# Segment sums on VectorE from transposed rows instead of on TensorE, with the average values and memory rows one token block later

## The chip, the core and the metric

The kernel runs on one core of a Trainium2 chip. Its engines work in parallel, each through its own instruction queue in order: TensorE (matmuls), VectorE, ScalarE, GpSimd, and SyncE, which here only issues DMA transfers (GpSimd issues some too). The metric is the device time of the whole kernel in microseconds (us). Tiles on the chip have 128 partitions; matmul results land in PSUM and are emptied from there by VectorE or ScalarE.

## What is computed

The input x has 2048 tokens of 1024 features. With xn = layernorm(x), the output is the sum of x, a recurrent attention over xn, and an MLP over xn:

```python
xn = _layernorm(x)
return x + _A_ref(xn, mem0, Wq, Wk, Wv, Wo, 32) + _B_ref(xn, w1, w2, w3, w4)
# _A_ref: 64 segments of 32 tokens, one after the other
mem = mem0                                  # 8 memory rows
for s in range(64):
    h = concat([mem, xs[s]])                # 40 rows: memory, then the segment
    o = attention(h @ Wq, h @ Wk, h @ Wv) @ Wo      # 32 heads of 128, causal mask on the segment
    mem = o[:8]; outs.append(o[8:])
# _B_ref: token-mixing MLP, then a plain one
h  = gelu(layernorm(xn) @ w1);  x1 = xn + shift(h) @ w2
return x1 + gelu(layernorm(x1) @ w3) @ w4   # w3: 1024 x 3584
```

The loop over segments is serial as written. The kernel breaks it by an approximation that it verifies at its end: a memory row attends to all 40 rows almost evenly, so the memory of the next segment is close to the average of the 40 values, projected by Wo. For that it needs, ahead of the attention, the sum over the 32 tokens of each segment of xn: 64 sums of 1024 features. From these come the average values (a product with Wv) and from them the memory rows (a product with Wo).

## The kernel before

Four stages follow each other, and TensorE's order is the order of the code (a manual schedule).

1. *First matmul of the token mixing* (lines 171 to 350; about 1.5 to 69 us). 16 tiles of 128 tokens, taken in pairs. For each tile VectorE makes statistics and a normalised copy `xn2`, a DMA transpose (`dma_trans`, L234) or TensorE (`pe_trans`, L252) turns it to features on partitions, and TensorE multiplies it with w1 (`stage1`, `w1_part`, L265; `single`, L294). `normalise_x` (L244, ScalarE) overwrites the loaded x by xn, in place. `seg_sums` (L257 to L261) runs two tiles behind it: it takes the tile's xn, 128 tokens on partitions, as stationary operand in 8 slices of 128 features, against a constant 128 x 4 matrix of zeros and ones (`segone`), which yields the sums of its four segments; ScalarE copies them to `xs`.
2. *Second matmul of the token mixing* (L357 to L386; 69 to 125 us): w2, the residual x1, its statistics, `xn3` and its transposes `xn3Ts` (four tiles of 512 tokens, in the buffers tagged x0 to x3). x1 goes to memory as `R1`.
3. *MLP* (L388 to L578; 125 to 528 us). A loop over four blocks `tb` of 512 tokens. Each has a first phase of 28 groups of 8 matmuls with w3 (L553; ScalarE empties PSUM with the gelu, L554), and a second phase of 8 groups of 28 matmuls with w4 (L571; VectorE empties PSUM, L572, by adding into `R1`). All groups of both phases share one ring of four PSUM tiles (`mm_tile`). `load_R1(n)` (L475) brings R1 and x of tile n back; GpSimd adds x to R1; VectorE makes xn of x (L481), and GpSimd stores xn to memory (`xn_d`, L482), from where the attention will load it transposed. The x tile of this comes from a ring of two buffers, tag `xt`.
   Between the groups, `filler(tb, ph, i)` runs the work of the average values: 16 chunks of 1 MB of weights, 8 of Wv (`psvb`, L425) and 8 of Wo (`psG`, L446), at the places of the dictionary `plan`. A chunk is loaded by SyncE when the one before it in its buffer has been used (buffer x0 for the Wv chunks; x0 and x1 for the Wo chunks). `xb` (L402, L403) holds the segment sums as the moving operand for Wv; its first column includes mem0. The last chunk ends in the memory rows `MZ` (L449), which the attention subtracts from x (`make_xm`, L517) and projects (`mem_proj`).
4. *Attention* (from L580; 528 us to the end): 32 steps of projections, scores, values, and the output projection (L834).

Of the kernel before, what the change touches and what calls it, by code (L numbers as in the profile page):

```python
# [13 lines left out]
BF16 = mybir.dt.bfloat16  # L14
F32 = mybir.dt.float32
I32 = mybir.dt.int32
ALU = mybir.AluOpType
ACTF = mybir.ActivationFunctionType
AX = mybir.AxisListType
PSUM = bass.MemoryType.PSUM  # L20

P = 128
S = 2048
D = 1024
KT = D // P
NT = S // P
# [5 lines left out]
M = 8  # L32
SEG = 32
# [3 lines left out]
NG = NSEG - 1  # L37
# [26 lines left out]
def kernel(  # L64
# [16 lines left out]
    nc = tc.nc  # L81
    x_v = A_x[0].rearrange("(n p) d -> p n d", p=P)
# [14 lines left out]
    xn_d = tc.dram_tile([S, D], BF16, name="xn_scratch")  # L97
    xn_v = xn_d.rearrange("(n p) d -> p n d", p=P)
# [3 lines left out]
    def const_tile(name, arr, dt=BF16, later=False):  # L102
        a = _bf(arr) if dt == BF16 else np.asarray(arr, np.float32)
        d = nc.inline_tensor(a, name=name)
        t = cpool.tile(list(arr.shape), dt, name=name + "_sb")
        load = lambda: nc.gpsimd.dma_start(t[:], d.ap())
        if later:
            return load, t
        load()
        return t  # L110
# [11 lines left out]
    load_segone, segone = const_tile("c_segone", segone_np, later=True)  # L122
# [14 lines left out]
    def aux_tile(shape, tag, name):  # L137
        return psum.tile(shape, F32, tag=tag, bufs=1, name=name)
# [4 lines left out]
    spec = specx.enter_context(tc.tile_pool(name="spec", bufs=1))  # L143
    xs = spec.tile([P, KT, NSEG], F32)
    xb = spec.tile([P, KT, NG], BF16)
    m0 = spec.tile([M, D], BF16)
    lnst = spec.tile([P, NT, 4], F32)

    rightx = main.enter_context(ExitStack())
# [14 lines left out]
    with ExitStack() as keepx:  # L164
        keep = keepx.enter_context(tc.tile_pool(name="keep", bufs=1))
        w2_sb = keep.tile([P, KT, D], BF16)
        xts = [keep.tile([P, D], BF16, name=f"x{n}") for n in range(NT)]
# [3 lines left out]
        with ExitStack() as p0:  # L171
            big = p0.enter_context(tc.tile_pool(name="p0big", bufs=1))
            ring = p0.enter_context(tc.tile_pool(name="p0ring", bufs=3))
# [69 lines left out]
            def normalise_x(n):  # L243
                nc.scalar.activation(xts[n][:], xts[n][:], ACTF.Identity, bias=nms.pop(n)[:], scale=lnst[:, n, 2:3])  # L244
# [9 lines left out]
                        w = 2 if n == 0 else 4  # L254
                        nc.scalar.copy(xn2Ts[n // 2][:, n % 2, 4 * h + q:4 * h + q + w, :], p3_[:, q:q + w, :])

            def seg_sums(n):  # L257
                ps = aux_tile([P, KT, 4], "AB"[n % 2], "psX")
                for k in range(KT):
                    nc.tensor.matmul(ps[:, k, :], xts[n][:, k * P:(k + 1) * P], segone[:], start=True, stop=True)  # L260
                nc.scalar.copy(xs[:, :, 4 * n:4 * n + 4], ps[:])  # L261

            def w1_part(g, co, ps, ks):
                for k in ks:
                    nc.tensor.matmul(ps, w1_sb[:, k, co * P:(co + 1) * P], xn2Ts[g][:, :, k, :], start=(k == 0), stop=(k == KT - 1))  # L265
                if ks[-1] == KT - 1:
                    nc.scalar.activation(hTB[:, co, 2 + g * 256:2 + g * 256 + 256], ps, ACTF.Gelu_apprx_tanh)
# [21 lines left out]
            def single(n, b):  # L289
                ps = mm_tile("ps1")[:].rearrange("p (c t) -> p c t", c=4)  # L290
                for c in range(4):
                    co = 4 * b + c
                    for k in range(KT):
                        nc.tensor.matmul(ps[:, c, :], w1_sb[:, k, co * P:(co + 1) * P], xn2Ts[n // 2][:, n % 2, k, :], start=(k == 0), stop=(k == KT - 1))  # L294
                gelu4(n, b, ps)
# [30 lines left out]
            ln_apply(4)  # L326
            dma_trans(4)
            single(3, 0)
            seg_sums(0)
            seg_sums(1)  # L330
            normalise_x(2)
            ln_stats(6)
            ln_apply(5)
# [3 lines left out]
            for g in range(2, NT // 2):  # L337
                nxt = [n for n in (2 * g + 2, 2 * g + 3) if n < NT]
                for n in nxt:
                    if 6 < n + 1 < NT:  # L340
                        ln_stats(n + 1)
                    ln_apply(n)
                    dma_trans(n)
                stage1(g, range(4))
                for n in (2 * g, 2 * g + 1):
                    seg_sums(n - 2)
                    normalise_x(n)
                stage1(g, range(4, KT))
            seg_sums(NT - 2)
            seg_sums(NT - 1)  # L350

        x3_pool = rightx.enter_context(tc.tile_pool(name="x3", bufs=1, side="right"))
        w3b_pool = rightx.enter_context(tc.tile_pool(name="w3b", bufs=1, side="right"))
# [3 lines left out]
        with ExitStack() as p2:  # L357
            ring = p2.enter_context(tc.tile_pool(name="p2ring", bufs=4))
            for n in range(NT):
                x1 = ring.tile([P, D], F32, tag="x1", bufs=6)  # L360
                st = ring.tile([P, 2, 6], F32, tag="st")
                for ch in range(2):
                    ps = mm_tile("ps2")
# [7 lines left out]
                a = ring.tile([P, 1], F32, tag="a")  # L371
# [17 lines left out]
    with ExitStack() as p3:  # L389
        big = p3.enter_context(tc.tile_pool(name="p3big", bufs=1))  # L390
        ring = p3.enter_context(tc.tile_pool(name="p3ring", bufs=3))
        w4t = []
        for c in range(7):
            t = big.tile([P, 4, D], BF16, name=f"w4_{c}")
# [3 lines left out]
        ps9 = aux_tile([P, KT, M + 1], "B", "ps9")  # L398
        for k in range(KT):
            nc.tensor.matmul(ps9[:, k, :], m0[:, k * P:(k + 1) * P], eye9[:], start=True, stop=True)  # L400
        nc.vector.tensor_copy(MZ[:, :, 0:M], ps9[:, :, 0:M])
        nc.vector.tensor_tensor(xb[:, :, 0:1], ps9[:, :, M:M + 1], xs[:, :, 0:1], op=ALU.add)  # L402
        nc.vector.tensor_copy(xb[:, :, 1:NG], xs[:, :, 1:NG])  # L403

        chunks = {}

        def load_chunk(c, slot):
            t = x3_pool.tile([P, 8 * 512], BF16, tag=f"x{slot}", name=f"chunk{c}")
            if c < 8:
                nc.sync.dma_start(t[:].rearrange("p (k e) -> p k e", k=KT), Wv_v[:, :, c * 512:(c + 1) * 512])  # L410
            else:
                nc.sync.dma_start(t[:].rearrange("p (h d) -> p h d", h=4), Wo_v[:, (c - 8) * 4:(c - 7) * 4, :])
            chunks[c] = t
# [37 lines left out]
        plan = {}  # L451
        slots = {}
        for i in range(4):
            plan[(0, 1, 2 * i + 1)] = i
            plan[(1, 0, 7 * i + 6)] = 4 + i
            plan[(1, 1, 2 * i + 1)] = 8 + i
            plan[(2, 0, 7 * i + 6)] = 12 + i
        for c in range(16):
            slots[c] = 0 if c < 8 else c % 2

        def filler(tb, ph, i):
            c = plan.get((tb, ph, i))
            if c is None:
                return
            use_chunk(c)
            nx = c + 2 if c >= 8 else c + 1
            if c == 7:
                load_chunk(8, slots[8])
                load_chunk(9, slots[9])
            elif c < 7 or nx < 16:  # L470
                load_chunk(nx, slots[nx])
# [3 lines left out]
        def load_R1(n):  # L475
            R1 = ring.tile([P, D], F32, tag="R1", name="R1")
            nc.sync.dma_start(R1[:], R1_v[:, n, :])
            xt = ring.tile([P, D], BF16, tag="xt", name="xt", bufs=2)
            nc.sync.dma_start(xt[:], x_v[:, n, :])
            nc.gpsimd.tensor_tensor(R1[:], R1[:], xt[:], op=ALU.add)  # L480
            nc.vector.tensor_scalar(xt[:], xt[:], lnst[:, n, 0:1], lnst[:, n, 2:3], op0=ALU.subtract, op1=ALU.mult)  # L481
            nc.gpsimd.dma_start(xn_v[:, n, :], xt[:])  # L482
            R1s[n] = R1

        A = {}
# [62 lines left out]
        for tb in range(4):  # L548
            for f in range(FT):
                ps = mm_tile("ps3")  # L550
                w3 = w3a if f < FH else w3b
                for k in range(KT):
                    nc.tensor.matmul(ps[:], w3[:, k, (f % FH) * P:(f % FH + 1) * P], xn3Ts[tb][:, :, k, :], start=(k == 0), stop=(k == KT - 1))  # L553
                nc.scalar.activation(h3T[:, f, :], ps[:], ACTF.Gelu_apprx_tanh)  # L554
                filler(tb, 0, f)
                if f == 20:
                    load_R1(tb * 4)
            if tb == 0:
                load_chunk(0, 0)
            if tb == 3:  # L560
                rightx.close()
                att_open()
            for j in range(4):
                n = tb * 4 + j
                if j < 3:
                    load_R1(n + 1)
                R1 = R1s.pop(n)
                for ch in range(2):
                    ps = mm_tile("ps4")
                    for f in range(FT):  # L570
                        nc.tensor.matmul(ps[:], h3T[:, f, j * P:(j + 1) * P], w4t[f // 4][:, f % 4, ch * 512:(ch + 1) * 512], start=(f == 0), stop=(f == FT - 1))  # L571
                    nc.vector.tensor_tensor(R1[:, ch * 512:(ch + 1) * 512], ps[:], R1[:, ch * 512:(ch + 1) * 512], op=ALU.add)  # L572
                    filler(tb, 1, 2 * j + ch)
                nc.gpsimd.dma_start(R_v[:, n, :], R1[:])
                if tb == 3 and j == 0:
                    att_prep()
# [288 lines left out]
    for i in range(NS):  # L865
        s = new_step(i)
        p = steps.get(i - 1)
# [67 lines left out]
        if last:  # L935
            b = s.b
# [31 lines left out]
    with tc.If(cond > 0):  # L968
        with ExitStack() as fctx:
# [17 lines left out]
            with tc.For_i(0, NSEG, 1) as i:  # L987
# [7 lines left out]
                for hg in range(8):  # L995
# [8 lines left out]
                    ps = fps.tile([P, 4, L], F32, tag="mm")  # L1004
# [4 lines left out]
                    ps = fps.tile([P, 4, L], F32, tag="mm")  # L1009
# [4 lines left out]
                    ps = fps.tile([P, 512], F32, tag="mm")  # L1014
# [33 lines left out]
                for ch in range(2):  # L1048
                    ps = fps.tile([P, 512], F32, tag="op")
# [44 lines left out]
```

## Time and profile before

| what | number |
|---|---|
| time, median of 3 runs (lowest to highest) | 1485.37 us (1484.79 to 1486.12) |
| span of the profiled execution | 1481.8 us |
| TensorE busy | 1474.5 us |
| VectorE, ScalarE, GpSimd busy | 502.1, 346.9, 206.3 us |
| granted TensorE clock | full speed throughout |
| share of the DMA engines, block 0's second phase (173.65 to 225.83 us) | 0.53 |

How to read it: TensorE is busy nearly all the time, so the shares of the other engines say how much room lies beside it. The chain of waits follows the end of the kernel back to the start, at each step to what released it. In the rows of groups, the first number after the bar is the busy time in us, the second the mean of one in ns, and then comes the idle time of the engine before these instructions and what ended it. "DMA to landing" is the time from the issue of a transfer to its completion. A busy record of one matmul is longer than its slot, since matmuls are pipelined; the slot is read from the chain.

### The profile page before, as it was taken

The numbers are of one execution on the slowest core, as the hardware profiler recorded it, in microseconds if no ns is written. First come the engines' busy times: TensorE is split into PE (matmuls) and PEld (weight loads), VectorE is DVE, ScalarE is ACT, GpSimd is POOL, SyncE is SP. The second block draws the span as 40 slices with busy tenths as digits, with TensorE's granted clock in tenths as the row PEclk, the third lists the DMA queues.
The fourth block names the chain that finished last, engine by engine and source line by source line (L and its number), as shares of the span: only waits on it lengthen the run. The fifth ranks groups of instructions, "written<-read, shape, count | busy, mean of one in ns | idle before, by whom it ended". The sixth has DMA issues, their size and how long they took to land.

```text
span 1481.8 us, 28303 instructions
## 1 busy us (share of the span) xinstructions
PE 1474.5 (100%) x12400; PEld 758.2 (51%) x12400; DVE 502.1 (34%) x1025; ACT 346.9 (23%) x887; POOL 206.3 (14%) x482
## 2 busy tenths in 40 slices
PE   9999999999999999999999999999999999999998
PEld 8844444444444456666544444444444444444444
DVE  8283010010110213435441454540255432253443
ACT  6633202103113023333310232220122220032220
POOL 6152131211120201111100000000000000000000
PEclk9999999999999999999999999999999999999999
DMA  8599653454120735474531364541345452244301
GB/s 219 140 287 245 239 192 100 163 175 154 56 107 8 232 131 186 158 212 159 177 106 57 119 171 143 157 143 54 103 148 167 143 157 72 66 141 155 109 21 54
DMA packets 189184, 208.39 MB, mean 141 GB/s; under 512 B 50168, under 2 KB 157832, under 8 KB 189056
## 3 DMA queue, kind: packets, MB, share of 16 engines
q1 hardware_dynamic: 180768, 178.82, 40.3%
q0 software_dynamic: 8288, 27.72, 5.1%
q8 instruction: 99, 1.62, 0.5%
q14 instruction: 29, 0.24, 0.0%
HBM read 170.07 MB, written 25.17 MB: 132 GB/s over the span
## 4 chain that ended last, share of the span: by engine, by line
PE 99%; DMA 0%; SPq 0%; DVE 0%; issue 0%
PE psK L634 15%; PE psV L643 15%; PE psP L834 15%; PE psQ L616 15%; PE ps L553 13%; PE ps L571 13%; PE ps L366 4%; PE ps L265 3%; PE psS L667 1%; PE psO L697 1%; PE psM L652 1%; PE psvb L425 1%; PE psG L446 1%; PE ps L294 0%; DMA x<-in_A_x_dram 0%; PE ps L280 0%
## 5 line engine op out<-in xcount | busy, mean ns | idle before, releaser
L834 PE MATMUL psP<-wo_sb,oX 128*128 128x512 bf16 (+1 forms) x1056 | 222.2, 373 | 0.0
L571 PE MATMUL ps<-w,hT_all 128*128 128x512 bf16 x896 | 195.0, 379 | 0.0
L634 PEld LDWEIGHTS <-w 128*128 128x128 bf16 x1280 | 125.1, 98 | 99.1
L616 PE MATMUL psQ<-xT,w 128*128 128x512 bf16 x768 | 170.4, 379 | 0.0
L643 PE MATMUL psV<-w,xT 128*128 128x512 bf16 x768 | 170.3, 379 | 0.0
L634 PE MATMUL psK<-xT,w 128*128 128x512 bf16 x768 | 169.7, 379 | 0.0
L834 PEld LDWEIGHTS <-oX 128*128 128x128 bf16 x1056 | 103.2, 98 | 117.1
L616 PEld LDWEIGHTS <-w 128*128 128x128 bf16 x1024 | 98.8, 98 | 115.9
L635 ACT CAST K<-psK 128x512 bf16<-128x512 f32 (+1 forms) x160 | 80.3, 502 | 303.7 <-PE psK L634 303.7
L623 DVE TENSOR_TENSOR Q<-psQ,QM 128x512 bf16<-128x512 f32 (+1 forms) x128 | 87.3, 685 | 166.3 <-PE psQ L616 107.9
L644 ACT CAST V<-psV 128x512 bf16<-128x512 f32 x128 | 74.9, 585 | 289.6 <-PE psV L643 289.5
L571 PEld LDWEIGHTS <-hT_all 128*128 128x128 bf16 x896 | 87.2, 98 | 103.8
L554 ACT ACTIVATE hT_all<-ps 128x512 bf16<-128x512 f32 x112 | 66.8, 597 | 283.5 <-PE ps L553 283.5
L643 PEld LDWEIGHTS <-xT 128*128 128x128 bf16 x768 | 74.2, 98 | 84.7
L553 PE MATMUL ps<-xn3T,w3a 128*128 128x512 bf16 x448 | 97.7, 379 | 0.0
L553 PE MATMUL ps<-xn3T,w3b 128*128 128x512 bf16 x448 | 97.7, 379 | 0.0
L702 DVE TENSOR_TENSOR oX<-psE,VM 128x128 bf16<-128x128 f32 x32 | 9.3, 291 | 215.2 <-PE psE L698 215.2
L709 DVE TENSOR_TENSOR oX<-psO,VM 128x96 bf16<-128x96 f32 (+2 forms) x256 | 82.0, 391 | 0.0
L840 DVE TENSOR_TENSOR ot<-psP,Rt 128x512 bf16<-128x512 f32 (+1 forms) x33 | 22.3, 675 | 167.7 <-PE psP L834 164.8
L553 PEld LDWEIGHTS <-w3b 128*128 128x128 bf16 x448 | 43.6, 98 | 51.9
L553 PEld LDWEIGHTS <-w3a 128*128 128x128 bf16 x448 | 43.4, 98 | 51.8
L481 DVE TENSOR_SCALAR xt<-xt,lnst 128x1024 bf16<-128x1024 bf16 x16 | 8.7, 545 | 180.3 <-POOL R L480 180.3
(161 smaller groups left out, 1259.0 us busy)
## 6 DMA issues: line engine op xcount, KB each, us to landing
w<-in_A_Wq_dram SPq DMA_DIRECT2D x32, 1024.0 KB, 5.4
w<-in_A_Wk_dram SPq DMA_DIRECT2D x32, 1024.0 KB, 5.3
w<-in_A_Wv_dram SPq DMA_DIRECT2D x32, 1024.0 KB, 6.6
R_scratch<-x POOLq DMA_DIRECT2D x16, 512.0 KB, 7.5
R<-R_scratch SPq DMA_DIRECT2D x16, 512.0 KB, 7.0
chunk<-in_A_Wv_dram SPq DMA_DIRECT2D x8, 1024.0 KB, 5.4
R_scratch<-R POOLq DMA_DIRECT2D x16, 512.0 KB, 4.2
chunk<-in_A_Wo_dram SPq DMA_DIRECT2D x8, 1024.0 KB, 6.3
```

The costliest lines, as they stand in the source:

```text
L366: nc.tensor.matmul(ps[:], hTB[:, k, o:o + P], w2_sb[:, k, ch * 512:(ch + 1) * 512], start=(k == 0), stop=(k == KT - 1))
L553: nc.tensor.matmul(ps[:], w3[:, k, (f % FH) * P:(f % FH + 1) * P], xn3Ts[tb][:, :, k, :], start=(k == 0), stop=(k == KT - 1))
L554: nc.scalar.activation(h3T[:, f, :], ps[:], ACTF.Gelu_apprx_tanh)
L571: nc.tensor.matmul(ps[:], h3T[:, f, j * P:(j + 1) * P], w4t[f // 4][:, f % 4, ch * 512:(ch + 1) * 512], start=(f == 0), stop=(f == FT - 1))
L616: nc.tensor.matmul(ps[:], w[:, k, hh * P:(hh + 1) * P], s.xm[:, k, 0:512], start=(k == 0), stop=(k == KT - 1))
L623: nc.vector.tensor_tensor(q3[:, j0:16, 0:SEG], p3_[:, j0:16, :], QM[:, 4 * s.hg + hh, z + j0:z + 16].unsqueeze(2).to_broadcast((P, 16 - j0 ...
L634: nc.tensor.matmul(ps[:, 0:c], w[:, k, hh * P:(hh + 1) * P], s.xm[:, k, h2 * c:(h2 + 1) * c], start=(k == 0), stop=(k == KT - 1))
L635: nc.scalar.copy(s.K[:, hh, h2 * c:(h2 + 1) * c], ps[:, 0:c])
L643: nc.tensor.matmul(ps[:], s.xm[:, k, m * P:(m + 1) * P], w[:, k, :], start=(k == 0), stop=(k == KT - 1))
L644: nc.scalar.copy(s.V[:, m, :], ps[:])
L709: nc.vector.tensor_tensor(oX[:, h0:h0 + hn, :].rearrange("p h (m c) -> p m h c", c=P)[:, m0:m1, :, SEG * j:SEG * (j + 1)], o4[:, 4 * m0:4 ...
L834: nc.tensor.matmul(ps[:, 0:w], oX[:, h, m * P:(m + 1) * P], wo_sb[:, h, cc], start=(h == 0), stop=(h == H - 1))
```

## The change

The segment sums leave the first stage and TensorE. Instead, xn is made and stored in the first block and a half of the MLP stage, by a new function `make_xn` for each of the 16 tiles (load x, normalise on VectorE, store from GpSimd), apart from `load_R1`, which keeps its own load of x for the sum with R1. When four tiles are stored, `load_sum(b)` brings those 512 rows back by one DMA transpose from SyncE, with features on partitions and tokens along the free axis, into the buffer x0, which is free once block 0's first phase has ended. There VectorE sums 32 tokens at a time (`tensor_reduce`, four instructions of two feature slices each per block of 512). `last_sum` makes `xb` and starts the first chunk load. The average values begin one token block later (block 1's second phase instead of block 0's), and all later chunks move with them; the last one now lies in block 3's first phase. `m0s` keeps mem0's column sum until `xb` is made. The places in the schedule are given by the dictionary `prep`, whose keys are block, phase and group; `filler` runs what is there ahead of a chunk.

```diff
-            def seg_sums(n):
-                ps = aux_tile([P, KT, 4], "AB"[n % 2], "psX")
-                for k in range(KT):
-                    nc.tensor.matmul(ps[:, k, :], xts[n][:, k * P:(k + 1) * P], segone[:], start=True, stop=True)
-                nc.scalar.copy(xs[:, :, 4 * n:4 * n + 4], ps[:])
...
-        nc.vector.tensor_tensor(xb[:, :, 0:1], ps9[:, :, M:M + 1], xs[:, :, 0:1], op=ALU.add)
-        nc.vector.tensor_copy(xb[:, :, 1:NG], xs[:, :, 1:NG])
+        nc.vector.tensor_copy(m0s[:], ps9[:, :, M:M + 1])
...
-            plan[(0, 1, 2 * i + 1)] = i
-            plan[(1, 0, 7 * i + 6)] = 4 + i
-            plan[(1, 1, 2 * i + 1)] = 8 + i
-            plan[(2, 0, 7 * i + 6)] = 12 + i
+            plan[(1, 1, 2 * i + 1)] = i
+            plan[(2, 0, 7 * i + 6)] = 4 + i
+            plan[(2, 1, 2 * i + 1)] = 8 + i
+            plan[(3, 0, 7 * i + 6)] = 12 + i
...
+        def make_xn(n):
+            xt = ring.tile([P, D], BF16, tag="xt", name="xt", bufs=2)
+            nc.sync.dma_start(xt[:], x_v[:, n, :])
+            nc.vector.tensor_scalar(xt[:], xt[:], lnst[:, n, 0:1], lnst[:, n, 2:3], op0=ALU.subtract, op1=ALU.mult)
+            nc.gpsimd.dma_start(xn_v[:, n, :], xt[:])
+
+        def load_sum(b):
+            sums[b] = x3_pool.tile([P, KT * 512], BF16, tag="x0", name=f"xTs{b}")
+            nc.sync.dma_start_transpose(sums[b][:].rearrange("p (k t) -> p k t", k=KT), xn_d[b * 512:(b + 1) * 512, :])
+
+        def seg_sums(b, k0):
+            nc.vector.tensor_reduce(xs[:, k0:k0 + 2, 16 * b:16 * b + 16], sums[b][:].rearrange("p (k s i) -> p k s i", k=KT, i=SEG)[:, k0:k0 + 2, :, :], axis=AX.X, op=ALU.add)
+
+        def last_sum():
+            nc.vector.tensor_tensor(xb[:, :, 0:1], m0s[:], xs[:, :, 0:1], op=ALU.add)
+            nc.vector.tensor_copy(xb[:, :, 1:NG], xs[:, :, 1:NG])
+            load_chunk(0, 0)
...
+        for n in range(6):
+            do(0, 0, 10 + 3 * n, make_xn, n)
+        for n in range(6, 14):
+            do(0, 1, n - 6, make_xn, n)
+        do(1, 0, 0, make_xn, 14)
+        do(1, 0, 3, make_xn, 15)
+        for b, (load, sumat) in enumerate((((0, 1, 1), [(0, 1, 4)] * 4), ((0, 1, 5), [(1, 0, 1)] * 2 + [(1, 0, 2)] * 2),
+                                           ((1, 0, 3), [(1, 0, 10 + t) for t in range(4)]), ((1, 0, 14), [(1, 0, 22 + t) for t in range(4)]))):
+            do(*load, load_sum, b)
+            for t, pos in enumerate(sumat):
+                do(*pos, seg_sums, b, 2 * t)
+        do(1, 0, 26, last_sum)
...
         def load_R1(n):
...
             nc.gpsimd.tensor_tensor(R1[:], R1[:], xt[:], op=ALU.add)
-            nc.vector.tensor_scalar(xt[:], xt[:], lnst[:, n, 0:1], lnst[:, n, 2:3], op0=ALU.subtract, op1=ALU.mult)
-            nc.gpsimd.dma_start(xn_v[:, n, :], xt[:])
             R1s[n] = R1
```

Also removed are the calls of the old `seg_sums` in the first stage and, at the end of block 0's first phase, `load_chunk(0, 0)`, which `last_sum` now does.

More of the change, by code (lines that the diff above doesn't have):

```diff
@@ L146 @@
     m0 = spec.tile([M, D], BF16)
+    m0s = spec.tile([P, KT, 1], F32)
     lnst = spec.tile([P, NT, 4], F32)
@@ L328 @@
             single(3, 0)
-            seg_sums(0)
-            seg_sums(1)
             normalise_x(2)
@@ L345 @@
                 for n in (2 * g, 2 * g + 1):
-                    seg_sums(n - 2)
                     normalise_x(n)
                 stage1(g, range(4, KT))
-            seg_sums(NT - 2)
-            seg_sums(NT - 1)
         x3_pool = rightx.enter_context(tc.tile_pool(name="x3", bufs=1, side="right"))
@@ L453, with do @@
         for i in range(4):
-            plan[(0, 1, 2 * i + 1)] = i
-            plan[(1, 0, 7 * i + 6)] = 4 + i
-            plan[(1, 1, 2 * i + 1)] = 8 + i
-            plan[(2, 0, 7 * i + 6)] = 12 + i
+            plan[(1, 1, 2 * i + 1)] = i
+            plan[(2, 0, 7 * i + 6)] = 4 + i
+            plan[(2, 1, 2 * i + 1)] = 8 + i
+            plan[(3, 0, 7 * i + 6)] = 12 + i
         for c in range(16):
             slots[c] = 0 if c < 8 else c % 2
+        sums = {}
+        def make_xn(n):
[12 more added lines that the diff above has]
+            load_chunk(0, 0)
+        prep = {}
+        def do(tb, ph, i, f, *a):
+            prep.setdefault((tb, ph, i), []).append((f, a))
+        for n in range(6):
[10 more added lines that the diff above has]
+        do(1, 0, 26, last_sum)
         def filler(tb, ph, i):
+            for f, a in prep.get((tb, ph, i), ()):
+                f(*a)
             c = plan.get((tb, ph, i))
@@ L557 @@
                     load_R1(tb * 4)
-            if tb == 0:
-                load_chunk(0, 0)
             if tb == 3:
```

## The prediction

> **What bounds the kernel now.** I read the page's chain of waits first, to see which engine carries the end.
>
> ```profile
> PE 99%; DMA 0%; SPq 0%; DVE 0%; issue 0%
> PE psK L634 15%; PE psV L643 15%; PE psP L834 15%; PE psQ L616 15%; PE ps L553 13%; PE ps L571 13%; PE ps L366 4%; PE ps L265 3%; PE psS L667 1%; PE psO L697 1%; PE psM L652 1%; PE psvb L425 1%; PE psG L446 1%; PE ps L294 0%; DMA x<-in_A_x_dram 0%; PE ps L280 0%
> ```
>
> TensorE is the chain, end to end: its own waits add up to 2.7 us, nearly all at the start. So a matmul that is removed is worth its slot, and every new wait of TensorE is lost in full. Nothing else counts. Next I took the chain in order of time, in the first stage and then around block 0 of the MLP.
>
> ```profile
> 22.27 0.38 PE psX L260 x16
> 22.65 0.47 PE psT L252 x8
> ...
> 28.44 0.38 PE psX L260 x16
> 28.82 7.01 PE ps L265 x64
> 35.83 0.38 PE psX L260 x16
> ```
>
> Two tiles' segment sums (16 matmuls of 4 columns) take 0.38 us of the chain, 24 ns each. The 164 ns that the record of one gives is latency, not its slot.
>
> ```profile
> 173.65 12.09 PE ps L571 x56
> 185.74 0.96 PE psvb L425 x32
> ...
> 224.87 0.96 PE psvb L425 x32
> 225.83 9.28 PE ps L553 x43
> ```
>
> Block 0's second phase (eight groups of 28 matmuls, 6.05 us each) carries four average-value groups of 0.96 us.
>
> Last, the rows that price what is added: VectorE's sums along the free axis and its normalisation (groups by form), a 512-row transpose (the answer for its line), and loads and stores of one tile (the page's DMA issues).
>
> ```profile
> L676 DVE TENSOR_REDUCE ss<-EQ 128x16 f32<-128x528 f32 x32 | 22.5, 703 | 2.7
> L481 DVE TENSOR_SCALAR xt<-xt,lnst 128x1024 bf16<-128x1024 bf16 x16 | 8.7, 545 | 180.3 <-POOL R L480 180.3
> L503 SPq DMA_TRANSPOSE xT<-xn_scratch x4: 3970/6436/8562, 479.0 to 1106.6; - x4
> DMA to landing us min/median/max: 6.0/8.6/12.1
> Rt<-R_scratch SPq DMA_DIRECT2D x32, 256.0 KB, 2.9
> xn_scratch<-xt POOLq DMA_DIRECT2D x16, 256.0 KB, 2.3
> ```
>
> [...] 528 elements 703 ns, 16 elements 170 ns (L813), so 1.04 ns an element. A bf16 one isn't there. [...] SyncE stood 55.3 us at L503 waiting for TensorE. [...] SyncE was held 3.97 us by the undisturbed one (landing 6.0) and up to 8.56 (landing 12.1) beside weight loads.
>
> **The change, part by part.**
>
> *Removed, first stage:* 8 pairs of segment sums x 0.38 = 3.04 us of the chain, and 16 ScalarE copies of 0.18 us, which are off it. Not all of it may come through: tile 9's transpose was issued at 31.1 and landed at 39.0, while its first matmul starts at 36.20 + 3.5 = 39.7. Three of the pairs lie ahead of that, so TensorE would arrive at 38.6 and wait 0.4 us. Later tiles land 1 us or more ahead. Net: -2.6, ends -3.0 and -2.5.
>
> *Moved one block later:* four average-value groups go from block 0's second phase to block 1's, and so on to block 3's first phase. Same matmuls, same chunk loads (5.4 us, 12 us apart), so nothing. The memory rows (L449, 0.68 us) are then written at the end of block 3's first phase; their first reader on the path, L517, waits anyway for the second group there, 12 us later.
>
> *Added on VectorE:* 16 reductions of 1024 bf16 elements, an estimated 703 + 496 x 1.04 = 1219 ns each, 4.9 us for a block's four; the 16 normalisations are only moved. In first phases TensorE doesn't wait for VectorE (ScalarE empties its PSUM), so they cost nothing there. In block 0's second phase VectorE empties PSUM (L572), and make_xn for tiles 6 to 13 and the sums of block 0 stand in its queue among those.
>
> *Added on SyncE:* 16 more loads of 256 KB and four transposes of 1 MB. Bandwidth is there: the DMA share in that phase is about 0.5 and 1 MB chunk loads leave it. The order is the matter, below.
>
> *Added wait:* the xt ring has two buffers, shared by load_R1 and make_xn, 20 uses in a row instead of 4 in this stretch. A use by make_xn holds its buffer for load 2.9 + VectorE 0.55 + hand-over 0.4 + store 2.3 (alone) to 4.5 (with R1 and xt loads in flight, seen at 399 us); a use by load_R1 for 3.6 to 4.1 (R1 ahead) + 2.12 of GpSimd. Two buffers thus yield a tile about every 3.3 to 4 us, starting when the w4 loads have landed, at 165.3 (last issue 149.7 + 15.6).
>
> I worked the queues through in program order, in the clock of the trace of before (load 2.9, with R1 3.8, store 2.4 or 3.0 to 4.3 where loads overlap, transpose 4.1 / 6.1). Tile 0 lands at 166.0; tile 5 is stored at 190; SyncE spends 191.5 to 195.6 on block 0's transpose; tile 7 is stored at 199.6, tile 9 at 211.4. Tile 10's load is issued at 211.5 and it is normalised at 215.1. The four sums end at 220.0. Only then may SyncE issue the second transpose (it reuses the buffer x0), 220.1 to 224.2. Tile 12's load stands behind it: 224.2, landed 227.1, normalised 227.7. Behind that on VectorE is the add that empties the last PSUM tile of the phase, done at 228.4. PSUM has four such buffers, so group 3 of block 1 needs that one. With the average-value groups gone, the phase ends at 173.65 + 8 x 6.05 = 222.0, and group 3 is due at 222.0 + 3 x 1.73 = 227.2. TensorE waits **1.3 us**. With loads at 3.2 it is 3.7; with stores of 2.4 throughout, 0; I take **2.0**.
>
> The range of that term: all transfers at their fastest, 0 with 2 us to spare; loads 3.2, stores 3.3 and transposes 5, 5.5; the median transpose row (6.4) as well, 8.3. The delay goes around the ring up to seven times, so small errors of a row are multiplied.
>
> *End of the new chain:* the last sums end at about 261, chunk 0 has landed at 267, its first use is due after the second group of block 1's second phase, at 284. Hidden, with 17 us to spare.
>
> Sum: -3.04 + 0.4 + 2.0 = -0.6 us, so 1484.7.
>
> **The rivals.**
>
> A, the forecast: the gain is mostly eaten by the short wait at the border of blocks 0 and 1. 1484.7, between 1482.9 and 1488.
>
> B, no new wait: the ring keeps up, and only the first stage shows. For it: SyncE and the rings are nearly idle then, as block 0's chunks no longer load beside them, and the fastest rows are those taken undisturbed. Against it: seven turns must all be fast. 1485.37 - 2.6 to 3.0 = 1482.6.
>
> C, the wait is long: stores stay at 3.3 or more and transposes at the median. For it: of the four transposes on record three took 8.5 us or more to land; reading back what was just stored adds hand-overs that I can't see. Against it: those three ran beside weight loads. Stall 6.5: 1489.2, slower.
>
> D, the sums come too late for chunk 0, and TensorE waits at its use in block 1. It takes 17 us more delay than I find; all four transposes at 12.1 landing would give most of it. A wait of 5 there on top of A: 1489.7.
>
> **How the numbers follow.** A 0.43, B 0.32, C 0.21, D 0.04. The bound of 0.2% is 2.97 us, so faster means below 1482.4: only B with no wait for tile 9, about half of B, plus little: 0.18. Slower means above 1488.3: C and D less their low ends, 0.23. Within: 0.59. The range from 1482.0 to 1489.3 leaves out a few in 100 below and about 12 in 100 above.
>
> **What would show it.** Right: psX gone from the chain, 7.01 us pieces of L265 joined, a wait of some tenths before tile 9's first matmul; in the waits of TensorE, one new line at the first-phase matmul of block 1 released by VectorE's add, about 2 us, at the fourth group; on SyncE the second transpose issued straight after VectorE's fourth sum; reductions of about 1.2 us. B is right if TensorE has no wait there and the end moved by 2.6 to 3.0. C if the wait is above 5 us. I'd be wrong altogether if the wait sits at psvb's first use (D), if a bf16 reduction is far from 1.2 us, or if the second phase of block 0 itself stalls, which I exclude since each of its groups has 18 us from its end until its buffer is due.

## The result and the profile after

The changed kernel takes 1494.4 us (median; 1492.07 to 1498.48), the kernel before beside it 1485.08 us: a ratio of 1.0065, 95% interval [1.0042, 1.0087]. It is 9.3 us slower, outside the predicted range.

The chain's shares (page, part 4) and TensorE's waits, of the kernel after; the columns of the second are us in total, times, longest:

```profile
PE 94%; DMA 2%; DVE 2%; issue 1%; SPq 1%; POOL 0%; DVEq 0%; POOLq 0%
```

```profile
PE ps L580 <- DVE R L597: 8.9, 2, 5.0
...
PE ps L260 <- DMA xn2T<-xn: 1.6, 2, 1.2
```

The chain was 99% TensorE before. The new line is the first: the matmuls with w3 (L580, L553 before) wait for the add that empties the last PSUM tiles of block 0's second phase (L597), at the border that the prediction named, for 8.9 us and in two pieces (3.9 and 5.0) where it said 2.0 in one. The last line is the first stage, waiting for a transpose. The chain in order of time (start, us, what), first the end of the first stage in the kernel before, then the first stage and the border in the kernel after:

```profile
65.75 3.51 PE ps L265 x32
69.27 0.38 PE psX L260 x16
69.64 10.38 PE ps L366 x48
```

```profile
26.69 6.97 DMA xn2T<-xn
33.80 35.09 PE ps L260 x320
68.89 0.22 PE ps L356
```

```profile
216.26 3.54 DMA xt<-in_A_x_dram
...
221.64 2.52 DVE xs L463 x3
...
225.02 1.20 DVE xs L463
226.22 0.60 DVE R L597
...
227.88 2.30 SPq L460
...
230.24 5.30 DMA xt<-in_A_x_dram
...
235.67 0.55 DVE xt L455
236.22 0.61 DVE R L597
...
236.87 44.84 PE ps L580 x200
```

The first wait ends with the add at 226.22, which stood behind the four sums (L463). Read the second from the bottom: TensorE starts when the add at 236.22 is done; that add stood behind the normalisation of tile 12 (L455), that behind tile 12's load, that behind SyncE's second transpose (L460), that behind the sums. It is the predicted chain of queues, link by link, only later and longer. One thing was not predicted. The 200 matmuls take 44.84 us; at the full rate (224 in 48.35 us in e10_ring3_1024 below) they would take 43.2. Stretches of the kernel after say why; the last three columns are granted clock, DMA share and GB/s:

```profile
225.00:230.00 5.00, 3.13 (x9) 1.09 (x9) 2.87 (x5) 0.00 (x0) 1.07 (x2) 0.66 0.52 116
230.00:236.00 6.00, 1.88 (x9) 0.78 (x8) 0.33 (x1) 1.19 (x2) 0.00 (x0) 1.00 1.04 296
236.00:238.00 2.00, 1.13 (x3) 0.41 (x3) 1.28 (x3) 0.00 (x0) 0.97 (x2) 0.64 0.21 80
238.00:240.00 2.00, 2.00 (x6) 0.76 (x5) 0.00 (x0) 0.00 (x0) 0.64 (x2) 0.51 0.74 272
```

After each of the two waits TensorE runs for some us at about half clock (0.51 in 238 to 240). The second costs 1.6 us by the count above. Two groups of 8 lie between the waits, from 226.8 to about 231.8: 5.0 us where 3.5 would do, so the first costs about as much. The two stretches at half clock last from 226.3 to 229.7 and from 236.6 to 240.0, 3.4 us each. Shorter waits than these two were followed by it too: in e6 and e15 below, waits of 2.4 us.

The balance of the two profiled runs, 1481.8 and 1492.6 us: the first matmul with w3 starts at 125.20 before and 124.43 after (-0.8), the waits are 8.9, the half clock some 3.2: +11.3, of +10.8 measured. So there are two misses: the border costs about 12 us and not 2, and the first stage gave 0.8 us (first matmul with w2 at 69.64 before, 68.89 after) and not 2.6.

### The profile page after: what moved, and what is told of

It is laid out like the page before. It is cut to its first block, busy times and chain, and to the rows that moved or that the text cites. A ratio compares the mean times of both kernels' runs of the same rounds, so it can differ in the third digit from the quotient of the medians.

```text
span 1492.6 us, 27953 instructions
## 1 busy us (share of the span) xinstructions
PE 1467.6 (98%) x12154; PEld 755.3 (51%) x12272; DVE 524.5 (35%) x1042; ACT 345.3 (23%) x871; POOL 205.7 (14%) x482
## 4 chain that ended last, share of the span: by engine, by line
PE 94%; DMA 2%; DVE 2%; issue 1%; SPq 1%; POOL 0%; DVEq 0%; POOLq 0%
PE psK L659 15%; PE psP L859 15%; PE psV L668 15%; PE psQ L641 15%; PE ps L580 13%; PE ps L596 11%; PE ps L356 4%; PE ps L260 2%; PE psS L692 1%; PE psO L722 1%; PE psM L677 1%; DMA xt<-in_A_x_dram 1%; DVE st L205 1%; PE psvb L414 1%; PE psG L435 1%
## 5 line engine op out<-in xcount | busy, mean ns | idle before, releaser
L859 PE MATMUL psP<-wo_sb,oX 128*128 128x512 bf16 (+1 forms) x1035 | 221.1, 372 | 1.1
L648 DVE TENSOR_TENSOR Q<-psQ,QM 128x512 bf16<-128x512 f32 (+1 forms) x128 | 87.2, 685 | 166.0 <-PE psQ L641 107.5
L580 PE MATMUL ps<-xn3T,w3a 128*128 128x512 bf16 x448 | 100.9, 387 | 8.9 <-DVE R L597 8.9
L580 PE MATMUL ps<-xn3T,w3b 128*128 128x512 bf16 x448 | 97.7, 379 | 0.0
L580 PEld LDWEIGHTS <-w3a 128*128 128x128 bf16 x448 | 44.1, 99 | 63.2 <-issue 13.3
L597 DVE TENSOR_TENSOR R<-ps,R 128x512 f32<-128x512 f32 x32 | 22.0, 689 | 137.8 <-PE ps L596 137.2
L580 PEld LDWEIGHTS <-w3b 128*128 128x128 bf16 x448 | 43.6, 98 | 51.9
```

Of the source, the lines that this page charges most:

```text
L648: nc.vector.tensor_tensor(q3[:, j0:16, 0:SEG], p3_[:, j0:16, :], QM[:, 4 * s.hg + hh, z + j0:z + 16].unsqueeze(2).to_broadcast((P, 16 - j0 ...
L859: nc.tensor.matmul(ps[:, 0:w], oX[:, h, m * P:(m + 1) * P], wo_sb[:, h, cc], start=(h == 0), stop=(h == H - 1))
```

## The experiments

Each run stands beside runs of the kernel before on the same chip; their median was 1484.6 to 1485.0 us throughout. The names in the code are those of the change.

### What makes the wait at the border

T1: the ring of two xt buffers, as predicted, only with longer turns. T2: the four sums on VectorE and the transpose behind them, by themselves. T3: the late start of the ring (171.5 us, worked out as 166.0), by itself.

**e1_ring3**, the changed kernel with three xt buffers (in `load_R1` too; the room for the third comes from xs, which takes m0's memory when that is free):

```diff
-            xt = ring.tile([P, D], BF16, tag="xt", name="xt", bufs=2)
+            xt = ring.tile([P, D], BF16, tag="xt", name="xt", bufs=3)
```

> The changed kernel with three xt buffers instead of two (xs shares the memory of m0 to make room). Theory T1 (the ring of two buffers, with the turns of load, normalisation and store, makes VectorE late for the last PSUM tile of block 0's second phase): a third buffer shortens the sequence of 20 uses by about a third, VectorE's fourth sum ends near 213 instead of 226 us, and TensorE has no wait at the border of blocks 0 and 1; then also no stretch at half clock. Time 1484.3 to 1485 (the first stage's small gain alone). Rival T2 (the four sums of 4.6 us and the transpose behind them on SyncE are enough by themselves): the wait stays above 5 us and the time above 1491. Rival T3 (the transfers of the stage before end about 5 us later than in the kernel before, and that alone makes the wait): with three buffers the start at 171 us is still late, half of the wait stays, about 1489.

Measured: 1485.39 us, ratio 1.0005 [0.9997, 1.0014]. No wait for L597 is left: a third buffer is enough to end it. The ring started at 169.6, nearly as late as in the changed kernel, so the late start alone doesn't make the wait either. TensorE still waits 2.8 us for xn2T in the first stage, whose gain doesn't show.

**e2_sums_late**, two buffers, but no sum and no second transpose within block 0's second phase:

```diff
-        for b, (load, sumat) in enumerate((((0, 1, 1), [(0, 1, 4)] * 4), ((0, 1, 5), [(1, 0, 1)] * 2 + [(1, 0, 2)] * 2),
-                                           ((1, 0, 3), [(1, 0, 10 + t) for t in range(4)]), ((1, 0, 14), [(1, 0, 22 + t) for t in range(4)]))):
+        for b, (load, sumat) in enumerate((((0, 1, 1), [(1, 0, 0)] * 4), ((1, 0, 3), [(1, 0, 8)] * 4),
+                                           ((1, 0, 9), [(1, 0, 15)] * 4), ((1, 0, 16), [(1, 0, 22 + t) for t in range(4)]))):
```

> The changed kernel, two buffers, with block 0's sums moved out of its second phase to the head of block 1's first phase, and the later transposes and sums moved back accordingly, so that neither VectorE's four sums nor SyncE's second transpose stand ahead of tiles 11 to 13. T1: the ring is still late, but 4.6 us of sums and some 4 us of SyncE are gone from ahead of tile 12; worked through with the durations of the changed kernel's trace the wait falls from 8.9 to 2.6 us, at the third and fourth group, and the time to 1487 to 1488.5. T2 (sums and transpose alone): no wait, 1484.3 to 1485. T3: as T1, no more than 4 us gained.

Measured: 1486.19 us, 1.0011 [1.0002, 1.0019], and no wait at the border either, as T2 has it, where T1 expected a shorter one. So the ring alone doesn't make it: the wait needs both, a slow ring and what stands between tile 10 and tile 12 in it. Here TensorE waits 3.2 us for xn2T.

### The other parts of the change, alone

**e4_pe_sums_stage2**, the kernel before with TensorE's sums moved from the first stage into the second: `seg_sums(n)` is called in the loop over tiles there.

> The kernel before with the same 128 matmuls of the segment sums moved from the first stage to the second (one tile's eight ahead of its matmuls with w2); nothing else is changed, TensorE does the same work. It measures what taking the sums out of the first stage yields there. If the first stage gives the whole slot (3.04 us, as in the prediction less 0.4), the time is that of before, 1485, at most 0.5 more. If TensorE, being earlier, runs into the normalisations and transposes of tiles 0 to 9, as the 3.6 us of waits in the changed kernel's first stage suggest, the second stage starts only 0.5 us sooner and the kernel is slower than before by about 2.5 us: 1487.6.

Measured: 1486.21 us, 1.001 [1.0002, 1.0019], 1.2 us more, between the two expectations; 0.9 of it is a new wait (TensorE for ScalarE's copy of the sums). The first stage did end earlier (its last matmul with w1 done at 67.6, before at 69.3) and had no wait for xn2T.

**e5_values_late**, the kernel before with only the `plan` of the average values one block later:

> The kernel before with nothing but the average values and memory rows one token block later (the dictionary of places and the first chunk load). All theories take this part at nothing: within 0.1% of before, 1484 to 1486, with no new wait of TensorE. If the later memory rows or the chunk loads in block 3 cost something at the start of the attention, it is slower by what TensorE waits there.

Measured: 1485.02 us, 1.0002 [0.9994, 1.001]. Moving them costs nothing, as predicted.

So the gain of the first stage is to be had (e4), and something else in the changed kernels eats it.

### Where the first stage's gain went

In the kernel before and e4, the transpose of tile 7 (issued at about 27 us) landed 5.1 to 5.4 us after its issue; in after, e1 and e2 after 7.0, 8.7 and 9.0 us. The diff has an innocent line, `m0s`, 32 bytes a partition, reserved ahead of every tile of the first stage: they all lie 32 bytes further on. The four runs that follow ask whether that does it.

**e6_before_shift32**: only the shift.

```diff
     m0 = spec.tile([M, D], BF16)
+    pad = spec.tile([P, KT, 1], F32)
```

> The kernel before with one unused tile of 32 bytes a partition (set once by GpSimd), so that every tile reserved after it lies 32 bytes further on, at addresses that are 32 and not 0 modulo 64, as in the changed kernel; nothing else is changed. Theory placement (the first-stage transposes, whose destination xn2T moves with it, land later at such addresses): the transposes of tiles 7 and 8 land 7 to 9 us after issue, against 4.0 to 5.1 us in the kernel before; TensorE waits 2 to 3 us on xn2T<-xn at one group of the first stage; 1487 to 1489 us. Rival (the transposes are late in the changed kernels because the segment sums no longer stand between the matmuls of that stage, so TensorE asks for each tile sooner): landing and waits as in the kernel before, 1485 us.

**e7_ring3_64**, **e8_after_64**, **e9_ring3_64_right**: `m0s` 64 bytes wide, with three buffers, with two, and with the other end of the memory shifted too.

> The changed kernel with three xt buffers in place of two (the sums' tile xs shares memory with m0s), and m0s 64 bytes a partition wide in place of 32, so that all later tiles lie at 0 modulo 64 again. Theory placement: no wait on xn2T<-xn over 1 us in the first stage, the transposes of tiles 7 and 8 land 4 to 6 us after issue, no wait at the border of the two phases, 1482 to 1483 us, narrow spread. Rival (removal of the sums): as e1_ring3, 1485.4 us with a wait of 2.8 us on xn2T.

> The changed kernel with m0s 64 bytes a partition wide in place of 32 and nothing else; the two xt buffers and so the wait at the border stay. Theory placement: 2.5 to 3 us less than the changed kernel, about 1491 us, or down to 1487 if the later loads into xt land sooner too and the wait at the border shrinks from 8.9 to 5 us. Rival: 1494 us, as the changed kernel, with a border wait of 8.9 us.

> As e7_ring3_64, with 32 more bytes reserved at the other end of the memory, so that the second stage's tiles and xn3T, which lie at 32 modulo 64 in all other kernels, lie at 0 modulo 64 too. Theory placement: the transposes of the MLP stage land sooner by a third or so; as TensorE doesn't wait for them, the time is that of e7_ring3_64 within 1 us (1482 to 1483 us). Rival (placement has no effect): 1485.4 us as e1_ring3, transposes as there.

Measured: e6 1486.41 us, 1.0007 [0.9999, 1.0016], tile 7's transpose 8.3 us, TensorE waits 2.4 us. e7 1485.87 us, 1.0005 [0.9995, 1.0015], transpose 9.3 us, wait 3.9. e8 1494.65 us, 1.0069 [1.0054, 1.0084], transpose 7.8. e9 1484.92 us, 1.0001 [0.9993, 1.0009], transpose 7.6. So the shift alone makes the transpose late in a kernel that has its sums (e6), against the rival; that it costs time is not clear from e6, whose interval includes 1, but from e12 and e15 below. But the remedy failed: 64 bytes aren't the measure. In e9 the transposes of the MLP stage, expected sooner by a third, landed as in e7 (median 6.7 us, 7.1 in e7, for the segment sums; 8.7 and 8.8 for the attention). The addresses themselves are in no trace: the runs show how far a tile was moved from where it lies in the kernel before.

**e10_ring3_1024**, **e11_after_1024**: `m0s` 1024 bytes wide, with three buffers and with two. **e12_before_shift128**, **e13_before_shift256**: as e6, with 128 and 256 bytes.

> The changed kernel with three xt buffers (xs sharing memory with m0) and m0s 1024 bytes a partition wide, so that the tiles of the first stage lie 1024 bytes away from where they lie in the kernel before: the same address modulo 1024 (e7_ring3_64 had restored it only modulo 64, and its transposes stayed late). Theory placement modulo more than 64: tile 7's transpose lands 4.8 to 5.4 us after issue (7.0 to 9.3 in the changed kernels so far), no wait on xn2T over 1 us in the first stage, 1482 to 1483 us, narrow spread. Rival (placement plays no part; the transposes are late because TensorE, without the sums, or the loads around them stand differently): 1485 to 1486 us as e1_ring3 and e7_ring3_64, a wait of 2 to 4 us on xn2T.

> The changed kernel itself, two xt buffers, with only m0s widened to 1024 bytes a partition: the first stage's tiles at the addresses of before modulo 1024. Theory placement: the first stage's gain comes back, 2 to 3 us less than the changed kernel, 1491 to 1492.5 us, with the wait at the border of the phases still there (5 to 9 us). Rival: 1494 us.

> The kernel before with an unused tile of 128 bytes a partition ahead of the first stage's tiles. If what counts is the address modulo 128, as before: 1484.8 us, tile 7's transpose lands in about 5 us, narrow spread. If it counts modulo 256 or more: as e6_before_shift32, 1486.4 us with a wide spread, tile 7's transpose at 7 to 9 us and TensorE waiting 2 us for it. Rival (any new unused tile does it, by what it adds to the schedule): as e6_before_shift32.

> The same with 256 bytes. If what counts is the address modulo 128 or 256: as the kernel before, 1484.8 us, tile 7's transpose at about 5 us. If modulo 512 or more, or if any unused tile does it: as e6_before_shift32, 1486.4 us, transpose at 7 to 9 us.

| kernel | place of xn2, modulo 256 | tile 7's transpose, us | time, us | ratio to before |
|---|---|---|---|---|
| e10_ring3_1024 | as before | 5.2 | 1482.22 | 0.9982 [0.9974, 0.9991] |
| e11_after_1024 | as before | 5.5 | 1490.97 | 1.0045 [1.0031, 1.0058] |
| e12_before_shift128 | 128 off | 7.7 | 1486.88 | 1.0018 [1.0011, 1.0024] |
| e13_before_shift256 | as before | 5.8 | 1484.62 | 0.9999 [0.9991, 1.0007] |

All four went as the theory says, with 256 as the measure. e10 is faster than both kernels. Its chain in the first stage and at the border:

```profile
24.93 42.13 PE ps L259 x384
...
67.33 10.74 PE ps L355 x49
...
214.49 4.91 PE ps L596 x22
219.40 48.35 PE ps L580 x224
```

The 384 matmuls with w1 stand in one piece, w2 starts at 67.33 (69.64 before), and block 1's first phase follows block 0's second phase without a gap.

Last, which tile: **e14_dest_only**, **e15_source_only**, **e16_others_only** put 128 unused bytes so that only xn2T (where the transpose writes), only xn2 (where it reads), or only the tiles of x, w1, w2 and the hidden rows are off. The lines shown are e15's; e14 has a second such tile ahead of xn2T, so that xn2 is moved by 256, and e16 has one ahead of all these tiles and one ahead of xn2T.

```diff
+                if n == 0:
+                    pads.append(ring.tile([P, KT, 4], F32, tag="padB", bufs=1, name="padB"))
                 xn2 = xn2s[n] = ring.tile([P, D], BF16, tag="xn2", name="xn2", bufs=4)
```

> The kernel before with two unused tiles of 128 bytes a partition around the first stage's xn2T: only the destination xn2T of the first-stage transposes lies 128 bytes off (128 modulo 256), the source xn2 lies at 0 modulo 256 again and everything else where it was. If the destination's address is what makes them late: as e12_before_shift128, 1486.9 us, tile 7's transpose in 7 us or more. If the source's or another tile's: 1484.6 us, about 5 us.

> The same with one unused tile between xn2T and xn2: only the source xn2 lies 128 bytes off. If the source's address is what makes the transposes late: 1486.9 us, tile 7's transpose in 7 us or more. If the destination's or another tile's: 1484.6 us, about 5 us.

> The kernel before with 128 unused bytes ahead of the first stage's tiles and 128 more ahead of xn2T: the tiles for x, w1, w2 and the hidden rows lie 128 bytes off, xn2T and xn2 at 0 modulo 256. If the transposes' own tiles matter: 1484.6 us, tile 7's transpose in about 5 us. If the tiles that are loaded beside them matter (x and w2): 1486.9 us, 7 us or more.

Measured: e14 1484.64 us, 1.0001 [0.9993, 1.001]; e15 1486.92 us, 1.0013 [1.0006, 1.0019]; e16 1484.4 us, 0.9998 [0.999, 1.0007]. Tile 7's transpose in e14 and then in e15:

```profile
L238 SPq DMA_TRANSPOSE xn2T<-xn x1: 1232/1232/1232, 26.7 to 26.7; - x1
...
DMA to landing us min/median/max: 5.2/5.2/5.2
```

```profile
L237 SPq DMA_TRANSPOSE xn2T<-xn x1: 1233/1233/1233, 26.8 to 26.8; - x1
...
  PE ps L268: 2.4, 1
...
DMA to landing us min/median/max: 8.4/8.4/8.4
```

It is the source. In all 18 traces tile 7's transpose took 4.8 to 5.8 us where xn2 was not moved or by 256 or 1024 bytes, and 7.0 to 9.3 in the others, where it was moved by 32, 64 or 128 bytes (modulo 256). Why such a source makes it late, no run shows.

The late transpose costs more than its wait. In e15 TensorE waits 2.4 us, and then come:

```profile
35.32 5.32 PE ps L268 x32
40.64 0.38 PE psX L263 x16
41.02 7.01 PE ps L268 x64
```

32 matmuls take 5.3 us where 3.5 is the full rate: the granted clock was 0.50 from 37 to 40. It was so in e6 (32 in 5.27 us, after 2.4) and e2 (64 in 8.81, after 3.2), but not in e1 (79 in 8.78, after 2.8). So the length of a wait doesn't decide by itself whether half clock follows; the last section has what the traces show of it.

### Which term of the border wait was too small

**e17_after_1024_early**, e11 with the first two tiles ahead of the loads of w4, which starts the ring sooner and leaves its turns:

```diff
+        make_xn(0)
+        make_xn(1)
         w4t = []
...
-        for n in range(6):
+        for n in range(2, 6):
             do(0, 0, 10 + 3 * n, make_xn, n)
```

> e11_after_1024 (two xt buffers, first-stage tiles back in place, 1491 us) with the first two make_xn issued ahead of the loads of w4 in place of 14 and 17 groups after them, so that the ring of xt starts some 10 to 20 us sooner. If the start of the ring behind the w4 loads is what made the border wait longer than 2 us: the wait is gone, 1482 to 1483 us, as e10_ring3_1024 with its third buffer. If the ring's own turns (held stores, GpSimd's add, transposes) set the wait: 3 us or more stay, 1487 us or more.

Measured: 1485.29 us (1481.42 to 1491.07 in 14 runs), 1.0005 [0.9995, 1.0016], between the two expectations. In the profiled run, the quickest one, there is no wait at the border and tile 12 is normalised at 224.1, where e11 has 230.1. So in that run the start is a lever of about 6 us, but it doesn't make two buffers safe: other runs took up to 10 us more. There is no profile of those, so that the border wait is what they have is likely and not shown.

## Why the prediction was wrong

The sum was -3.04 + 0.4 + 2.0. Its form was right. The step that failed is its last term, the added wait: 2.0 us, where TensorE waited 8.9 (5.2 with the first stage's tiles in place). Beside it two terms were put at nothing without a reason: that the first-stage transposes would land later, and that a wait is followed by matmuls at half clock. The experiments price the whole: e10 holds the gain (-2.4 us), the placement is worth 2.8 us with three buffers (e1 +0.4, e10 -2.4 against before) and about 3 with two (+9.3, e11 +6.35), the third buffer's lack 8.75 (e11 against e10), half clock included in both. -2.4 + 2.8 + 8.75 = 9.15, of 9.3.

**Removed, first stage: right in size, but eaten.** e10 gained 2.4 where 2.6 was worked out. That the transposes of the changed kernel would land as those of the kernel before was taken for granted, and the added `m0s` line broke it: TensorE waited 1.6 us for xn2T in after. This is the first missing term. Waits for VectorE ahead of TensorE's own transposes (psT) were 2.0 us in after and 0.4 in before too; but they were 1.7 in e5, which is as before up to there, so they are not put down to the change.

**Moved one block later: right**, nothing (e5).

**Added on VectorE: right.** The rows of the sums tile xTs, kernel after:

```profile
L463 DVE TENSOR_REDUCE xs<-xTs x16: 1202/1208/1220, 221.6 to 270.6; 128x32 f32<-128x1024 bf16 x16
L460 SPq DMA_TRANSPOSE xTs<-xn_scratch x4: 3767/4412/5382, 196.8 to 261.2; - x4
```

1.208 us each, predicted 1.219; that bf16 would cost what f32 does per element was the author's estimate, and it held. The transposes hold SyncE for 3.8 to 5.4 us, the fast end or somewhat above.

**Added wait: the right place and mechanism, the wrong size.** e11, with its tiles in place, is the clean comparison:

```profile
PE ps L580 <- DVE R L597: 5.2, 1, 5.2
...
225.32 4.65 DMA xt<-in_A_x_dram
...
231.30 30.76 PE ps L580 x131
```

The time at which each step is done or, where it says so, begun:

| step | worked out | e11 | after |
|---|---|---|---|
| normalisation of the first tiles begins | 166.0 | 165.2 | 171.5 |
| the four sums end | 220.0 | 221.1 | 226.2 |
| tile 12's load is issued | 224.2 | 225.3 | 230.2 |
| tile 12 has landed | 227.1 | 230.0 | 235.5 |
| the last add is done | 228.4 | 231.3 | 236.8 |
| TensorE waits | 1.3 | 5.2 | 8.9 |

Up to the load of tile 12 the working was within about a us of e11 after some ten turns. Then three errors add up to the 3.9 us between 1.3 and 5.2. The load of tile 12 took 4.65 us, where the row of a lone load, 2.9, was used (1.75), though the second transpose, issued 4.2 us ahead of it, was still under way (those of after landed 5.9 us or more after issue); in after, where the same load took 5.30 us, the transfers together moved 311 GB/s in that time. The sums ended 1.1 late. And TensorE asked at 226.1 and not 227.2: the gain of the first stage stood in the sum but not in the clock in which the queues were worked out, so a faster TensorE met the same transfers sooner. In after the loads of w4 were issued at 147.5 (before 142.5, e11 141.4), and so the ring began 6 us later than in e11. That start varies: it was 145.9 in e5, which is as before up to there. The wait varies too: the quickest run of e8, again with two buffers, has 3.9. The range of the term, 0 to 8.3, takes in e11's 5.2; the 8.9 of after lies above it, and the 2.0 taken was at its lower end.

**The granted clock: missing.** A wait was costed at its length. In e11 the 5.2 us were followed by 131 matmuls in 30.8 us; at the full rate they take 28.3, so 2.5 us more were lost. Rival C, "the wait is long", had the mechanism and a wait of 6.5, and with the half clock (1.6 to 3.2) and the lost gain (1.8) would have said about 1493 to 1494.

**Of the signs named**, psX left the chain, the reductions took 1.2 us and the second transpose followed the fourth sum at once; "a wait above 5 us" was the sign of C, and it was there.

## What to carry to other kernels

When a removed operation makes the bounding engine arrive sooner, work the other queues out again in the new clock: what was hidden by a few us becomes a wait, and a wait of TensorE can cost more than its length. Here half clock, worth another 1.5 to 2.5 us, followed waits of 2.4 us (e6, e15) to 5.2 (e11), though not one of 2.8 (e1). Read a diff for what it moves in memory too: a new small tile shifts every tile behind it, and here tile 7's transpose, with its source moved by 32, 64 or 128 bytes modulo 256, landed after 7.0 to 9.3 us and not after 4.8 to 5.8. A ring that one more user joins wants one more buffer, above all where an engine that empties PSUM stands behind it in its queue.

## What was not expected of the hardware

**The source's address.** With its source moved by 128 bytes, the first-stage transpose of tile 7 (256 KB) landed 8.4 us after issue (e15) and not after 5.1 (before) to 5.8 (e13, moved by 256); with 32 and 64 bytes it was late too (8.3 in e6, 7.8 in e8). With the destination alone moved by 128 it landed after 5.2 (e14).

**When the granted clock was halved.** In the two traces that have it twice, the starts and ends of half clock lie whole multiples of an estimated 3.41 us apart. In e8 there are two such stretches, one in each stage; the last three columns are again clock, DMA share and GB/s, and a clock between 0.5 and 1 says at what point of the half microsecond it changed:

```profile
35.00:35.50 0.50, 0.50 (x6) 0.43 (x4) 0.44 (x3) 0.00 (x0) 0.00 (x0) 0.78 1.41 451
38.50:39.00 0.50, 0.50 (x6) 0.39 (x4) 0.50 (x2) 0.00 (x0) 0.50 (x2) 0.81 1.05 365
233.00:233.50 0.50, 0.50 (x3) 0.17 (x2) 0.18 (x1) 0.00 (x0) 0.03 (x1) 0.75 0.00 0
236.50:237.00 0.50, 0.50 (x3) 0.25 (x2) 0.00 (x0) 0.09 (x1) 0.00 (x0) 0.83 1.08 246
```

So it went down at an estimated 35.28 and 233.25 and up at 38.69 and 236.67: 3.41 and 3.42 us, and 197.97 between the two falls, 58 times 3.413. The four changes in after (226.31, 229.72, 236.55 and 239.96, estimated in the same way) are 3.41, 6.83 and 3.41 us apart. In the stretch of 3.41 us ahead of each fall in after, e6, e7, e8, e11 and e15 TensorE was busy for 1.34 us (e15) or less, in after for 0.06 and 0.00; after stretches with 2.09 (e7), 2.16 (after) and 2.40 (e8) the clock stayed up. So of e15's wait of 2.4 us an estimated 2.07 lay in one such stretch. That e1's 2.8 passed because it was divided between two is the author's estimate, and not shown.

**VectorE's normalisation beside GpSimd's add.** In the kernel after, GpSimd's add of x to R1 and VectorE's normalisation, which took 0.55 us where no such add ran beside it (timelines: start, us):

```profile
219.31 2.12 POOL L509 TENSOR_TENSOR R<-R,xt 128x1024 f32<-128x1024 f32 x1 [4.34 <-DMA xt<-in_A_x_dram]
```

```profile
219.93 1.79 DVE L455 TENSOR_SCALAR xt<-xt,lnst 128x1024 bf16<-128x1024 bf16 x1 [5.73 <-DMA xt<-in_A_x_dram]
221.64 4.58 DVE L463 TENSOR_REDUCE xs<-xTs 128x32 f32<-128x1024 bf16 x4
```

It ends at 221.72, 0.3 us after the add (221.43), and so in three more places (1.36, 1.13 and 1.77 us). Why it ends only then, no run shows. It put 1.2 us into the ring's turn just ahead of the sums; in e11, where the same normalisation took 1.77 us, that is about what the sums were late (1.1).
